# Scatters into expert bins: from pairs without a wait to one transfer at a time

## The chip, the cores and the metric

The kernel runs on one core of one Trainium2 chip. The metric is the device time in microseconds (us), taken as the median of several executions; the version before the change has 756.64 us, from three runs between 754.47 and 756.89.

## The reference

Two stages follow each other. The first filters each of 8 sequences of 2496 rows and 256 columns along its length in the frequency domain. The second sends each of the 19,968 filtered rows to one of eight experts.

```python
X = np.fft.rfft(x, axis=1)
y = np.fft.irfft(X * (filt_r + 1j * filt_i)[None], n=2496, axis=1)   # (8, 2496, 256)
x = y.reshape(19968, 256)
logits = x @ w_gate + modality_bias[modality_id]                     # 8 experts
e_idx = np.argmax(logits, axis=1)
gate_w = softmax(logits)[arange, e_idx]
for e in range(8):
    mask = e_idx == e
    h = np.maximum(x[mask] @ w1[e], 0.0)                             # 256 -> 1024
    out[mask] = gate_w[mask, None] * (h @ w2[e])                     # 1024 -> 256
```

## The kernel before

**The filter.** A sequence is a *group* `g`, 0 to 7. Its transform is cut into three stages of matrix products with data going through DRAM between them: `stage1` (input rows to `b1_d`), `stage2` (the other factor, the filter, and its inverse, to `b2_d`) and `stage3` (the last factor, into the tile `yw`). GpSimd loads the inputs (`load_x`, L125, four loads for a group), SyncE stores the results of the first two stages (L228, L454) and loads them again (L415, L422).

**The routing.** `stage3` leaves the rows of a group in `yw`, as 20 columns of 128 rows (the last two columns of 96), 520 bytes for a row: 256 values in 16 bits, the row's number and its gate. `count` and `place` compute the expert of each row and its place `pos` in that expert's bin. `yw` and `pos` have two buffers each. L463 writes the row numbers into a new `yw`.

**The bins.** `scatter(g, k)` writes two columns with two indirect transfers of GpSimd (L561), each taking the place of 128 rows from `pos`, into the DRAM tensor `bins_d`. Scatters are declared free of dependencies on each other and on loads written ahead of them. A load of the bins that is written after a scatter does wait for it.

**The experts.** The bins are read in 85 blocks of 256 rows of one expert. `load` brings a block in (`xs`, SyncE, L635), three blocks ahead; `turn` copies the expert's first weights (L651) and transposes the block (L661); `up` (L672, L676) and `down` (L684) compute it in four steps each, `down` of one block beside `up` of the next. After the last step of `down`, VectorE scales the result into `osb` (L691, three buffers), and GpSimd writes the rows to the output with two indirect transfers (L694). A call of `moe.step()` makes one step, so every fourth call issues an output pair.

**The order.** One loop over *slots* `n` writes the program. In each slot each stage of the groups that are under way advances by one piece; a group starts 14 slots after the one before it. Then one pair of scatters follows where a group is waiting for it in `to_bins`, and 2.25 expert steps on average. Twenty scatters thus take ten slots, and in the eleventh the group's blocks are opened for the experts. Groups have 1, 10, 10, 10, 9, 10, 10 and 25 blocks. The last group's blocks are opened after ends of bins have been padded (`pad_bins`, L709, SyncE). When the slots end, the rest of the blocks is computed without anything else beside it. The instructions of each engine are then ordered by when they are ready in the program's own planning, where a pin does not say otherwise: `behind("out", 1)` keeps a scatter behind the last output transfer written ahead of it. A pin is an order on the engine's queue and no wait.

```python
        if to_bins:
            g, k = to_bins[0]
            if k < NPY:
                scatter(g, k)
                to_bins[0][1] += 1
            else:
                if g == B - 1:
                    pad_bins()
                moe.open(tabs[g], KR[g], g == B - 1)
                to_bins.pop(0)
```

Of the kernel before, what the change touches and what calls it, by code (L numbers as in the profile page):

```python
# [17 lines left out]
IOA = bass.IndirectOffsetOnAxis  # L18
# [10 lines left out]
def kernel(  # L29
# [395 lines left out]
    def stage2(g, k):  # L425

        s = k * EV
        if s < NS:
            ps = pp.tile([P, EV, D], F32, tag="ps")
            for i in range(EV):  # L430
                nc.tensor.matmul(ps[:KB, i, :], lhsT=w2m[:, s + i, :], rhs=st[g]["t2", s // SCH][:, s % SCH + i, :],  # L431
                                 start=True, stop=True)
        if k > 0:
            s_ = s - EV
            p1, p2 = st[g]["p"]
            pz = pp.tile([P, EV, D], F32, tag="ps")
            for i in range(EV):
                nc.tensor.matmul(pz[:KB, i, :], lhsT=a1m[:, s_ + i, :], rhs=p1[:, i, :], start=True, stop=False)  # L438
                nc.tensor.matmul(pz[:KB, i, :], lhsT=a2m[:, s_ + i, :], rhs=p2[:, i, :], start=False, stop=True)  # L439
        if s < NS:  # L440
            sl = slice(s, s + EV)
            xf = rp.tile([KB, EV, D], BF16, tag="xf")
            nc.scalar.copy(xf, ps[:KB])  # L443
            p1 = rp.tile([KB, EV, D], BF16, tag="p1")
            nc.vector.tensor_mul(p1, xf, g1[:, sl, :])  # L445
            nc.vector.tensor_mul(xf, xf, g2[:, sl, :])  # L446
            st[g]["p"] = (p1, xf)
        if k > 0:
            kk = k - 1
            if kk % 2 == 0:  # L450
                st[g]["z"] = rp.tile([KB, 2, EV, D], BF16, tag="z", bufs=2, name="z")
            nc.scalar.copy(st[g]["z"][:, kk % 2], pz[:KB])  # L452
            if kk % 2 == 1:
                nc.sync.dma_start(b2_d[g, s - 2 * EV:s].rearrange("s p c -> p s c"),  # L454
                                  st[g]["z"].rearrange("p a b d -> p (a b) d"))

    def stage3(g, k):

        u0 = k * EV
        if k == 0:  # L460
            yw = yp.tile([P, NY, RW], I32, tag="yo", name="yo")
            st[g]["yw"] = yw
            nc.gpsimd.tensor_single_scalar(yw[:, :, DW:DW + 1], tok, g * S, op=ALU.add)  # L463
            lg = sp.tile([P, NY, E], F32, tag="lg", bufs=2)
            st[g]["lg"] = lg
            nc.vector.tensor_mul(lg, mids[:, g, :, None].to_broadcast([P, NY, E]),
                                 biasd[:, None, :].to_broadcast([P, NY, E]))
            nc.vector.tensor_add(lg, lg, bias0[:, None, :].to_broadcast([P, NY, E]))
        yo = st[g]["yw"].bitcast(BF16)
        if k < NPY:  # L470
            t0 = TCH[k // 3][0]
            t4 = st[g]["t4", k // 3]
            ps = pp.tile([P, EV, D], F32, tag="ps")
            for i in range(EV):
                a, b = divmod(u0 + i, 3)
                t, tc_, c0 = (4 * a + b, 4 * a + 3, b * KC) if u0 < NYF else (4 * NYG + i, 4 * NYG + 1, 0)
                nc.tensor.matmul(ps[:KA, i, :], lhsT=wbm, rhs=t4[:, t - t0, :], start=True, stop=True)  # L477
                nc.tensor.matmul(ps[KA:P, i, :], lhsT=wbm[:, c0:c0 + KC], rhs=t4[:, tc_ - t0, :],  # L478
                                 start=True, stop=True)

        ub, uc = u0 - EV, u0 - 2 * EV
        if k > 0:
            lt = pp.tile([P, 2 * D], F32, tag="ps")
            pT = lt[:, 0:D].bitcast(BF16).rearrange("p (i a q) -> p i a q", i=EV, a=DC)
            psL = lt[:, D:D + EV * E].rearrange("p (i e) -> p i e", e=E)
        if 0 < k <= NPY:
            for i in range(EV):
                for dc in range(DC):
                    nc.tensor.transpose(pT[:, i, dc, :], yo[:, ub + i, dc * P:(dc + 1) * P], ident)  # L489
        if k > 1:  # L490
            yT = st[g]["yT"]
            for i in range(EV):
                for dc in range(DC):
                    nc.tensor.matmul(psL[:, i, :], lhsT=yT[:, i, dc, :], rhs=wg[:, dc, :],
                                     start=(dc == 0), stop=(dc == DC - 1))
        if 0 < k <= NPY:
            st[g]["yT"] = sp.tile([P, EV, DC, P], BF16, tag="yT", bufs=2, name="yT")
            nc.vector.tensor_copy(st[g]["yT"], pT)  # L498
        if k < NPY:
            dst = yo[:, u0:u0 + EV, 0:D]  # L500
            if k % 2:
                nc.scalar.activation(dst, ps, AF.Copy, scale=1.0 / S)
            else:
                nc.vector.tensor_scalar_mul(dst, ps, 1.0 / S)
        if k > 1:
            lg = st[g]["lg"]
            nc.vector.tensor_add(lg[:, uc:uc + EV], lg[:, uc:uc + EV], psL)
# [46 lines left out]
        nc.vector.reduce_sum(ssum, lg, axis=AX.X)  # L554
        nc.vector.reciprocal(yw[:, :, DW + 1].bitcast(F32), ssum)

    def scatter(g, k):
        for t in range(k * EV, (k + 1) * EV):
            rows = P if t < NYF else KA
            with behind("out", 1):  # L560
                ins = nc.gpsimd.indirect_dma_start(  # L561
                    out=bins_d[:, :], out_offset=IOA(ap=st[g]["pos"][:rows, t:t + 1], axis=0),
                    in_=st[g]["yw"][:rows, t, :], in_offset=None)

            free_of(ins, "bins")
            free_of(ins, "bin_reads")
            tc.add_to_no_dep_group("bins", ins.ins)

    def free_of(ins, group):
        tc.declare_no_dep(ins.ins, group=group, reason="disjoint rows")  # L570
# [48 lines left out]

    binv = bins_d.rearrange("(n p i) d -> n p i d", p=P, i=NI)  # L620

    marks = {"ld": [], "up": [], "w1": [], "out": []}

    def behind(what, n):

        m = marks[what]
        return tc.issue_after(m[-n]) if len(m) >= n else nullcontext()
# [39 lines left out]
    def up(b, q):  # L667
        hps = hp.tile([P, FQ, NI * P], F32, tag="hps")
        for k in range(FQ):
            ft = q * FQ + k  # L670
            for dc in range(DC):
                mm = nc.tensor.matmul(hps[:, k, :], lhsT=b["w1"][:, dc, ft * P:(ft + 1) * P],  # L672
                                 rhs=b["xT"][:, dc].rearrange("p i t -> p (i t)"),
                                 start=(dc == 0), stop=(dc == DC - 1))
        marks["up"].append(mm.ins)
        nc.scalar.activation(b["hT"][:, q * FQ:(q + 1) * FQ, :], hps, AF.Relu)  # L676

    def down(b, q):
        if q == 0:
            b["ops"] = op.tile([P, NI, D], F32, tag="ops", bufs=2, name="ops")  # L680
        for k in range(FQ):
            ft = q * FQ + k
            for i in range(NI):
                nc.tensor.matmul(b["ops"][:, i, :], lhsT=b["hT"][:, ft, i * P:(i + 1) * P],  # L684
                                 rhs=w2sb[:, ds(b["ej"], 1), ft, :],
                                 start=(ft == 0 and i == 0), stop=(ft == FT - 1 and i == NI - 1))
        if (q + 1) * FQ == FT:
            osb = ep.tile([P, NI, D], F32, tag="osb", bufs=3)
            gate = b["meta"][:, :, 1:2].bitcast(F32)
            for i in range(NI):  # L690
                nc.vector.tensor_scalar_mul(osb[:, i, :], b["ops"][:, i, :], gate[:, i, :])  # L691
            for i in range(NI):
                kw = dict(bounds_check=N - 1, oob_is_err=False) if b["last"] else {}
                ins = nc.gpsimd.indirect_dma_start(  # L694
                    out=out[:, :], out_offset=IOA(ap=b["meta"][:, i, 0:1], axis=0),
                    in_=osb[:, i, :], in_offset=None, **kw)
                marks["out"].append(ins.ins)
                free_of(ins, "outs")
                tc.add_to_no_dep_group("outs", ins.ins)

# [69 lines left out]
    owed = 0.0  # L770


    GAP = NP + 1
    OFF2 = NP + 3
    OFF3 = OFF2 + NS // EV + 1 + 3
# [2 lines left out]
    while True:  # L778
# [9 lines left out]
        for g in range(B):  # L788
# [7 lines left out]
            if k == NPY + 3:  # L796
                place(g)
                tabs[g] = table(KR[g], g == B - 1)
                to_bins.append([g, 0])
        if to_bins:  # L800
            g, k = to_bins[0]
            if k < NPY:
                scatter(g, k)
                to_bins[0][1] += 1
            else:
                if g == B - 1:
                    pad_bins()
                moe.open(tabs[g], KR[g], g == B - 1)
                to_bins.pop(0)
        if (n - NP) % 4 == 0 and (n - NP) // 4 < E:  # L810
            load_w((n - NP) // 4)
        owed += STEPS
        while owed >= 1:
            owed -= 1
            moe.step()
        n += 1
        if not to_bins and n > (B - 1) * GAP + OFF3 + NPY + 4:
            break
# [32 lines left out]
```

## Time and profile before

| | |
|---|---|
| Median of the runs | 756.64 us |
| The profiled execution's own time | 879.74 us |
| Its span, first to last instruction | 878.0 us |
| Mean granted TensorE clock in it | 0.811 of full speed |
| Busy: TensorE, VectorE, ScalarE, GpSimd | 650.8, 385.7, 387.3, 367.7 us |
| Scatters (L561) | 160, 979 ns each on GpSimd |
| Output transfers (L694) | 170, 989 ns each on GpSimd |
| First scatter, last scatter issued | 151.3 us, 706.3 us |

The profile comes from one execution, which took 123 us longer than the median run. Durations are read from it and compared inside it; a time for the runs needs the step from one to the other. PE is TensorE's matrix products, PEld its weight loads, DVE VectorE, ACT ScalarE, POOL GpSimd and SP SyncE. A row of the groups gives line, engine, operation and tiles, the count, then busy time and mean duration in ns, then the idle time of the engine just ahead of such instructions and what ended most of it. SPq is SyncE's DMA queue, which does no arithmetic.

### The profile page before, as it was taken

To read this page: it belongs to the slowest core of one execution; us is meant where nothing else is said; L and a number is where in the kernel's file an instruction comes from. 1 tells how busy PE (TensorE), PEld (TensorE's weight loads), DVE (VectorE), ACT (ScalarE), POOL (GpSimd) and SP (SyncE) were. 2 spreads that over 40 slices of the span, in tenths; PEclk is the share of its full clock that TensorE was granted. 3 is DMA by queue.
4 is the path that set the end of the run, shared out by engine and by line. 5 is a ranking of instruction groups with operands and counts; after the bars stand their busy time and mean duration, and the time that the engine had idled before them with its cause. 6 is when DMAs were issued, how large, how long until landed. Compare 5 with 4: busy or idle time off the path is not lost.

```text
span 878.0 us, 15948 instructions
## 1 busy us (share of the span) xinstructions
PE 650.8 (74%) x4886; PEld 497.7 (57%) x4886; DVE 385.7 (44%) x1248; ACT 387.3 (44%) x695; POOL 367.7 (42%) x413
## 2 busy tenths in 40 slices
PE   1463678697596787787956886877694679999996
PEld 1352446465365556565744674665473457777775
DVE  5431235346255434553733464454253224444442
ACT  1553335345254444463724543452242235555553
POOL 5131201625505433544345345435546544444444
PEclk9985555557579878897969899897897769999998
DMA  8799986566465446454533343342222223222320
GB/s 154 162 223 211 225 176 159 130 139 173 105 149 149 121 100 160 119 149 100 168 110 112 100 115 117 88 127 71 70 73 95 95 79 101 94 92 92 96 64 1
DMA packets 92696, 106.80 MB, mean 122 GB/s; under 512 B 12708, under 2 KB 75754, under 8 KB 92460
## 3 DMA queue, kind: packets, MB, share of 16 engines
q0 software_dynamic: 29120, 50.75, 24.8%
q1 hardware_dynamic: 63496, 55.03, 23.9%
q8 instruction: 44, 0.72, 0.4%
q14 instruction: 36, 0.29, 0.1%
HBM read 71.87 MB, written 54.31 MB: 144 GB/s over the span
## 4 chain that ended last, share of the span: by engine, by line
PE 23%; issue 17%; POOL 8%; another core or an unknown queue 4%; DMA 4%; DVE 3%; ACT 2%; POOLq 0%; SPq 0%; DVEq 0%; ACTq 0%
PE hps L672 7%; PE ops L684 6%; POOL out_dram L694 6%; DMA out_dram<-osb,meta 2%; PE ps L478 2%; POOL bins_d L561 2%; PE ps L477 2%; PE lt L489 1%; DMA bins_d<-yo,pos_i 1%; ACT hT L676 1%; PE ps L431 1%; PE pT L661 1%; PE pz L439 1%; PE pz L438 1%
## 5 line engine op out<-in xcount | busy, mean ns | idle before, releaser
L676 ACT ACTIVATE hT<-hps 128x512 f16<-128x512 f32 x340 | 197.4, 597 | 282.1 <-PE hps L672 131.6
L694 POOL DMA_INDIRECT out_dram<-osb,meta x170 | 168.1, 989 | 269.0 <-DVE osb L691 220.3
L672 PE MATMUL hps<-xT,w 128*128 128x256 f16 x1360 | 231.4, 293 | 32.8 <-ACT hT L676 16.5
L684 PE MATMUL ops<-w2sb,hT 128*128 x1360 | 226.6, 289 | 9.8 <-issue 9.3
L561 POOL DMA_INDIRECT bins_d<-yo,pos_i x160 | 156.7, 979 | 58.3 <-issue 47.3
L684 PEld LDWEIGHTS <-hT 128*128 128x128 f16 x1360 | 141.2, 104 | 45.2 <-issue 18.4
L672 PEld LDWEIGHTS <-w 128*128 128x128 f16 x1360 | 131.9, 104 | 61.2 <-issue 24.8
L225 ACT CAST t<-ps 96x512 f16<-96x512 f32 x104 | 59.7, 583 | 92.5 <-PE ps L222 31.6
L651 DVE COPY w<-w1sb 128x2048 f16 x85 | 59.2, 697 | 63.4 <-PE ops L684 46.7
L477 PE MATMUL ps<-t,wbm 96*96 96x256 f16 x160 | 56.8, 355 | 40.4 <-ACT t L225 18.8
L662 DVE COPY xT<-pT 128x512 f16<-128x512 f16 x85 | 35.9, 423 | 112.2 <-remote 39.9
L445 DVE TENSOR_TENSOR p<-xf,g 104x512 f16<-104x512 f16 x96 | 40.6, 423 | 96.4 <-ACT xf L443 80.3
L691 DVE TENSOR_SCALAR osb<-ops,meta 128x256 f32<-128x256 f32 x170 | 74.9, 477 | 15.6 <-PE ops L684 9.4
L222 PE MATMUL ps<-xt,w1m 96*96 96x256 f16 x208 | 53.3, 358 | 36.0 <-DVE w1m L205 16.7
L125 POOL DMA_DIRECT2D xt<-in_x_dram x32 | 18.9, 590 | 143.4 <-PE ps L222 117.4
L431 PE MATMUL ps<-t,w2m 104*104 104x256 f16 x192 | 48.4, 344 | 40.4 <-issue 12.0
L498 DVE COPY yT<-lt 128x512 f16<-128x512 f16 x80 | 33.8, 422 | 94.2 <-remote 43.5
L438 PE MATMUL pz<-p,a1m 104*104 104x256 f16 x192 | 62.4, 338 | 16.1 <-ACT t L225 5.9
L452 ACT CAST z<-pz 104x512 f16<-104x512 f32 x96 | 56.7, 590 | 34.5 <-PE pz L439 9.5
L443 ACT CAST xf<-ps 104x512 f16<-104x512 f32 x96 | 56.4, 587 | 23.2 <-PE ps L431 15.5
L439 PE MATMUL pz<-xf,a2m 104*104 104x256 f16 x192 | 62.9, 341 | 1.3 <-DVE xf L446 1.1
L489 PE MATMUL lt<-ident,yo 128*128 128x128 f16 x320 | 40.2, 264 | 24.4 <-ACT xf L443 16.6
(185 smaller groups left out, 632.1 us busy)
## 6 DMA issues: line engine op xcount, KB each, us to landing
xs<-bins_d SPq DMA_DIRECT2D x85, 130.0 KB
t<-b_d SPq DMA_DIRECT2D x24, 416.0 KB
b_d<-z SPq DMA_DIRECT2D x48, 208.0 KB
xt<-in_x_dram POOLq DMA_DIRECT2D x24, 384.0 KB
b_d<-t SPq DMA_DIRECT2D x48, 192.0 KB
t<-b_d SPq DMA_DIRECT2D x24, 384.0 KB
w1sb<-in_moe_w_dram POOLq DMA_DIRECT2D x8, 512.0 KB
w2sb<-in_moe_w_dram POOLq DMA_DIRECT2D x8, 512.0 KB
```

The source lines that it names most:

```text
L225: nc.scalar.copy(st[g]["t1"][:, k % 2], ps[:KA])
L431: nc.tensor.matmul(ps[:KB, i, :], lhsT=w2m[:, s + i, :], rhs=st[g]["t2", s // SCH][:, s % SCH + i, :], start=True, stop=True)
L438: nc.tensor.matmul(pz[:KB, i, :], lhsT=a1m[:, s_ + i, :], rhs=p1[:, i, :], start=True, stop=False)
L439: nc.tensor.matmul(pz[:KB, i, :], lhsT=a2m[:, s_ + i, :], rhs=p2[:, i, :], start=False, stop=True)
L477: nc.tensor.matmul(ps[:KA, i, :], lhsT=wbm, rhs=t4[:, t - t0, :], start=True, stop=True)
L561: ins = nc.gpsimd.indirect_dma_start(out=bins_d[:, :], out_offset=IOA(ap=st[g]["pos"][:rows, t:t + 1], axis=0), in_=st[g]["yw"][:rows, t, ...
L651: cp = nc.vector.tensor_copy(b["w1"].rearrange("p a f -> p (a f)"), w1sb[:, ds(ej, 1)].rearrange("p o a f -> p (o a f)"))
L672: mm = nc.tensor.matmul(hps[:, k, :], lhsT=b["w1"][:, dc, ft * P:(ft + 1) * P], rhs=b["xT"][:, dc].rearrange("p i t -> p (i t)"), start=(d ...
L676: nc.scalar.activation(b["hT"][:, q * FQ:(q + 1) * FQ, :], hps, AF.Relu)
L684: nc.tensor.matmul(b["ops"][:, i, :], lhsT=b["hT"][:, ft, i * P:(i + 1) * P], rhs=w2sb[:, ds(b["ej"], 1), ft, :], start=(ft == 0 and i == ...
L691: nc.vector.tensor_scalar_mul(osb[:, i, :], b["ops"][:, i, :], gate[:, i, :])
L694: ins = nc.gpsimd.indirect_dma_start(out=out[:, :], out_offset=IOA(ap=b["meta"][:, i, 0:1], axis=0), in_=osb[:, i, :], in_offset=None, **kw)
```

## The change

Each scatter call now issues one column, and each scatter gets a dependency on the indirect transfer written just ahead of it, a scatter or an output transfer (`follow`, over the list `marks["sc"]`): it is issued only when that transfer has landed. Outputs enter the list but get no such dependency themselves. The scatters of a slot are spread: one at its head and one after each expert step that issued no output, at most two in a slot. From the slot on in which the last group is placed, the limit is 20. The list `marks["pe"]` is filled by three places and read by none.

```diff
-    def scatter(g, k):
-        for t in range(k * EV, (k + 1) * EV):
-            rows = P if t < NYF else KA
-            with behind("out", 1):
-                ins = nc.gpsimd.indirect_dma_start(
-                    out=bins_d[:, :], out_offset=IOA(ap=st[g]["pos"][:rows, t:t + 1], axis=0),
-                    in_=st[g]["yw"][:rows, t, :], in_offset=None)
...
+    def scatter(g, t):
+
+        rows = P if t < NYF else KA
+        with behind("out", 1):
+            ins = nc.gpsimd.indirect_dma_start(
+                out=bins_d[:, :], out_offset=IOA(ap=st[g]["pos"][:rows, t:t + 1], axis=0),
+                in_=st[g]["yw"][:rows, t, :], in_offset=None)
+
+        free_of(ins, "bins")
+        free_of(ins, "bin_reads")
+        tc.add_to_no_dep_group("bins", ins.ins)
+        follow(ins)
+
+    def follow(ins):
+
+        if marks["sc"]:
+            tc.add_manual_dep(ins.ins, marks["sc"][-1].name,
+                              mybir.DependencyInfo(mybir.DependencyClass.Sync, mybir.DependencyReason.DATA),
+                              reason="one in flight")
+        marks["sc"].append(ins.ins)
...
-    marks = {"ld": [], "up": [], "w1": [], "out": []}
+    marks = {"ld": [], "up": [], "w1": [], "out": [], "pe": [], "sc": []}
...
                 marks["out"].append(ins.ins)
+                marks["sc"].append(ins.ins)
...
+    def pace(left):
+
+        if to_bins and left:
+            g, t = to_bins[0]
+            if t < NY:
+                scatter(g, t)
+                to_bins[0][1] += 1
+                left -= 1
+            else:
+                if g == B - 1:
+                    pad_bins()
+                moe.open(tabs[g], KR[g], g == B - 1)
+                to_bins.pop(0)
+        return left
...
+        left = 2 if n < (B - 1) * GAP + OFF3 + NPY + 3 else NY
+        left = pace(left)
         if (n - NP) % 4 == 0 and (n - NP) // 4 < E:
             load_w((n - NP) // 4)
         owed += STEPS
         while owed >= 1:
             owed -= 1
+            outs = len(marks["out"])
             moe.step()
+            if len(marks["out"]) == outs:
+                left = pace(left)
```

More of the change, by code (lines that the diff above doesn't have):

```diff
@@ L430, in stage2 @@
             for i in range(EV):
-                nc.tensor.matmul(ps[:KB, i, :], lhsT=w2m[:, s + i, :], rhs=st[g]["t2", s // SCH][:, s % SCH + i, :],
-                                 start=True, stop=True)
+                mm = nc.tensor.matmul(ps[:KB, i, :], lhsT=w2m[:, s + i, :],
+                                      rhs=st[g]["t2", s // SCH][:, s % SCH + i, :], start=True, stop=True)
+            marks["pe"].append(mm.ins)
         if k > 0:
@@ L477, in stage3 @@
                 nc.tensor.matmul(ps[:KA, i, :], lhsT=wbm, rhs=t4[:, t - t0, :], start=True, stop=True)
-                nc.tensor.matmul(ps[KA:P, i, :], lhsT=wbm[:, c0:c0 + KC], rhs=t4[:, tc_ - t0, :],
-                                 start=True, stop=True)
+                mm = nc.tensor.matmul(ps[KA:P, i, :], lhsT=wbm[:, c0:c0 + KC], rhs=t4[:, tc_ - t0, :],
+                                      start=True, stop=True)
+            marks["pe"].append(mm.ins)
         ub, uc = u0 - EV, u0 - 2 * EV
@@ L555, in place @@
         nc.vector.reciprocal(yw[:, :, DW + 1].bitcast(F32), ssum)
-    def scatter(g, k):
-        for t in range(k * EV, (k + 1) * EV):
-            rows = P if t < NYF else KA
-            with behind("out", 1):
-                ins = nc.gpsimd.indirect_dma_start(
-                    out=bins_d[:, :], out_offset=IOA(ap=st[g]["pos"][:rows, t:t + 1], axis=0),
-                    in_=st[g]["yw"][:rows, t, :], in_offset=None)
-            free_of(ins, "bins")
-            free_of(ins, "bin_reads")
-            tc.add_to_no_dep_group("bins", ins.ins)
+    def scatter(g, t):
[14 more added lines that the diff above has]
+        marks["sc"].append(ins.ins)
     def free_of(ins, group):
@@ L675, in up @@
         marks["up"].append(mm.ins)
+        marks["pe"].append(mm.ins)
         nc.scalar.activation(b["hT"][:, q * FQ:(q + 1) * FQ, :], hps, AF.Relu)
@@ L799 @@
                 to_bins.append([g, 0])
[L800 to L809, printed above, removed]
+        left = 2 if n < (B - 1) * GAP + OFF3 + NPY + 3 else NY
+        left = pace(left)
         if (n - NP) % 4 == 0 and (n - NP) // 4 < E:
```

## The prediction

> **What bounds the kernel now.** I read the busy line of the page first, then the windows by stage, then the rows of the two indirect transfers, then GpSimd's and SyncE's waits.
>
> ```profile
> PE 650.8 (74%) x4886; PEld 497.7 (57%) x4886; DVE 385.7 (44%) x1248; ACT 387.3 (44%) x695; POOL 367.7 (42%) x413
> ...
> L694 POOL DMA_INDIRECT out_dram<-osb,meta x170 | 168.1, 989 | 269.0 <-DVE osb L691 220.3
> ...
> L561 POOL DMA_INDIRECT bins_d<-yo,pos_i x160 | 156.7, 979 | 58.3 <-issue 47.3
> ```
>
> No engine is full: TensorE leads with 74%, GpSimd (POOL) is at 42%. A scatter into the bins (L561) holds POOL 0.98 us and is preceded by nothing but "issue" (0.30 us each): today it waits for no transfer. The windows (busy us of PE, PEld, DVE, ACT, POOL, each with a count; then clock, DMA share, GB/s) show where PE is not fed:
>
> ```profile
> 500.00:600.00 100.00, 77.41 (x659) 61.61 (x658) 54.71 (x189) 45.27 (x81) 44.72 (x47) 0.91 0.38 112
> 600.00:660.00 60.00, 45.12 (x360) 32.43 (x358) 24.54 (x77) 19.17 (x34) 31.48 (x33) 0.83 0.22 69
> 660.00:712.00 52.00, 27.84 (x194) 20.45 (x193) 15.75 (x55) 12.74 (x22) 30.22 (x31) 0.71 0.29 92
> 712.00:800.00 88.00, 84.09 (x742) 69.47 (x740) 40.91 (x103) 46.71 (x82) 39.48 (x42) 0.98 0.29 92
> ```
>
> While the last group is scattered (660 to 712) PE is busy 27.8 of 52 us; after the last scatter, 84 of 88. So scatters already set PE's pace there. The link is SyncE's (SPq) wait: a block's load reads the bins and waits until every scatter written ahead of it in the program has landed. The waits of SPq, then the chain in order of time (start, us, what), first around the third group's end, then in the last group:
>
> ```profile
> SPq L635 <- DMA bins_d<-yo,pos_i: 71.9, 20, 8.0
> ```
>
> ```profile
> 331.67 6.99 DMA bins_d<-yo,pos_i
> ...
> 342.40 2.33 DMA xs<-bins_d
> ...
> 345.40 1.04 PE hps L672 x4
> ```
>
> ```profile
> 670.95 2.28 DMA bins_d<-yo,pos_i
> ...
> 673.50 0.97 POOL out_dram L694
> ```
>
> Twenty loads waited 71.9 us for scatters; in the middle piece the load, and then PE, wait for one. The last piece gives the price: 2.28 us from issue to landing, and POOL goes on 0.27 us later (673.23 to 673.50). POOL's timeline shows today's spacing:
>
> ```profile
> 357.44 1.21 POOL L561 DMA_INDIRECT bins_d<-yo,pos_i  x1 [1.20 <-DVE m L594]
> 358.95 0.97 POOL L561 DMA_INDIRECT bins_d<-yo,pos_i  x1 [0.30 <-issue]
> 360.22 0.97 POOL L561 DMA_INDIRECT bins_d<-yo,pos_i  x1 [0.30 <-issue]
> 361.50 0.97 POOL L561 DMA_INDIRECT bins_d<-yo,pos_i  x1 [0.30 <-issue]
> 362.77 1.02 POOL L694 DMA_INDIRECT out_dram<-osb,meta  x1 [0.30 <-issue]
> 364.10 0.97 POOL L694 DMA_INDIRECT out_dram<-osb,meta  x1 [0.31 <-issue]
> 365.38 0.97 POOL L561 DMA_INDIRECT bins_d<-yo,pos_i  x1 [0.30 <-issue]
> ```
>
> Issue to issue is 1.27 us, so about two are in flight. In the trace's packets, a scatter's last data packet ends 1.88 us after issue in the quicker quarter, 2.30 us on the mean of 160.
>
> **What the Trainium skill says.** "DMA: Bandwidth & Descriptors", section "Anatomy of one DMA — SWDGE (gpsimd) path", gives about 2.0 us fixed plus bytes/436e3 for a GpSimd DMA, most of it the write receipt. For a scatter (128 rows of 520 bytes, 66,560) that is 2.15 us; the trace has 2.28, and agrees. For an output transfer (131,072 bytes) it is 2.30; the chain has 3.58 us (from 719.07), and the measurement is used. The same page, "Rules for kernel authors", says to issue early and wait on the semaphore late, so that the fixed cost overlaps. The change does the reverse for these transfers.
>
> **The change part by part.**
>
> 1. *The wait.* Nothing is added in instructions or bytes; 160 scatters get a wait on POOL. Behind another scatter, the distance grows from 1.27 to 2.28 + 0.27 = 2.55 us at best; with the mean packet end (2.30 + 0.40 + 0.27) 2.97. I take 2.8. Behind an output, 3.58 + 0.27 = 3.85 us from that output's issue, unless other POOL work fills it.
> 2. *POOL in one steady group.* A group is 14 slots; from the first scatter of the third group (270.3) to that of the eighth (664.4) it takes 78.8 us in the profiled execution. The median run is 756.64/879.74 = 0.860 of that execution, so 67.8 us at its pace. Today POOL needs 20 × 1.27 + 16 outputs × 1.27 + 4 input loads × 0.87 = 49 us. After: ten slots hold 22.5 steps, so 5.6 output pairs, and 14.4 scatters follow a scatter. 14.4 × 2.8 = 40.3; the 5.6 scatter-pair-scatter stretches take 3 × 1.27 = 3.8 us each where the pair goes into a wait that exists anyway (21.3); the remaining 2.3 pairs and the input loads 9.3. Sum **71 us**. It fits into 78.8 and exceeds 67.8 by 3. If each wait behind an output is met in full, 5.6 × (2 × 1.27 + 3.85) = 35.8 replaces 21.3: **85 us**.
> 3. *What queues behind.* Behind a waiting scatter on POOL stand the outputs (three osb buffers let PE run about three blocks ahead) and the input loads at L125. On the other side, SPq's block loads wait for the scatters, and behind them on SPq stand the FFT's stores (L228, L454) and loads (L415, L422). Scatters take 61.6 of a group's 71 us where they had ten slots, 48 us at the median's pace: 13 us late, under three blocks' 26 us, but the 20 waits of 71.9 us lengthen. I price a steady group at 5 us (3 of POOL, 2 of SPq) in a range of 0 to 17; five groups: **+25**.
> 4. *The first two groups.* No outputs are mixed in: today 27.4 and 25.5 us of scatters, after 20 × 2.8 = 56. The first block and the next ten come some 29 us later each. Cover: the FFT work, which can run ahead. From 0 to 29 each; I take 10: **+20**.
> 5. *The last group.* No cover: PE has 27.8 us of work in 52. Today its scatters run from 664.4 to 707.2. After, about 15.5 × 2.8 + 4 × 3.8 = 59 us, 16 more, with one block less passed meanwhile (+4): **+20**, between 0 and 30.
> 6. *The placing.* One per step instead of a pair per slot, none after a step that issues outputs; in the last group up to three per slot. No instruction is added; the rate stays two per slot elsewhere, so nothing by itself. The matmul marks are read by nothing: zero.
>
> Sum: +65 us. Against the profiled execution (879.74) items 4 and 5 stay and item 3 shrinks to 2 per group, some +50, near 930. Against the median of the runs: 756.6 + 65 = **822 us**. Own range 785 to 860.
>
> **The rivals.**
>
> *Full waits.* Every scatter behind an output holds POOL idle until that output has landed. Groups need 85 us against 67.8: +17 × 5, with 29 × 2 at the start less some cover (30) and 30 at the end: +145, **900 us**. For: the diff puts outputs into the chain. Against: outputs are free to be ordered ahead of a waiting scatter; the trace shows POOL work moved to where it is ready (L463 stands right behind a group's last scatter).
>
> *Hidden.* The order of the queues already spaces the scatters out, and blocks are in stock: **757 us**. For: POOL is idle 58% of the span. Against: SPq's 71.9 us of waits, and the bursts at 1.27 us.
>
> *Faster.* Bursts of four scatters hold back an output pair by 4 × 1.27 = 5.1 us, which in 660 to 712 leaves PE 24 us idle. If spread scatters let outputs pass, and the last group's blocks open three slots earlier, up to those 24 us come back: **733 us**. It decides if the scatters of the last group end no later than today, so at under 43/20 = 2.1 us each; the cheapest wait measured is 2.55.
>
> *The wait isn't there.* If a landed transfer is never ahead, distances stay 1.27 and the time 757. The explicit dependency speaks against.
>
> **How the numbers follow.** Slow-down of item sums 0.60; full waits 0.22; hidden or no wait 0.06; faster 0.12. A measurement of this kernel tells about 0.3% (2.3 us) from no change; so faster 0.12, same 0.05, slower 0.83. The range takes in the likeliest case, hidden at its lower edge and full waits at its upper: 755 to 905.
>
> **What would show it.** Right: in POOL's timeline scatters 2.5 to 3 us apart, idle before them ended by the transfer ahead; L561's idle time up from 58 to some 250 us; SPq L635 waiting well over 72 us for bins; the last group's scatters over 55 us. Wrong: scatters still 1.27 us apart, or spaced with SPq's wait for bins unchanged and the 660 to 712 stretch no longer. Full waits would show as output-landing waits ahead of scatters summing to over 100 us.

## The result, and the profile after

The changed kernel takes 765.01 us (762.88 to 767.98, four runs) against 756.76 us (754.47 to 757.99, four runs): a ratio of 1.0115, 95% interval 1.0073 to 1.0157. A second comparison on another occasion gave 1.0162 (1.0107 to 1.0217), so the change costs 1 to 2%, some 8 to 13 us. That is slower, as forecast, but by only an eighth to a fifth of the 65 us in the sum.

The profiled execution that the prediction reads (879.74 us) ran at another pace than the timed runs of the same kernel. A second profile of that kernel took 748.95 us with a span of 747.2 us. All comparisons of profiles below are with the second one, which is called "before, second profile". What slowed the first is not known; its effect on the forecast is told further down.

The busy line and the rows of the two indirect transfers, changed kernel:

```profile
PE 617.4 (81%) x4886; PEld 485.3 (63%) x4886; DVE 381.2 (50%) x1248; ACT 394.8 (52%) x695; POOL 372.8 (49%) x413
...
L706 POOL DMA_INDIRECT out_dram<-osb,meta x170 | 167.2, 984 | 162.2 <-DVE osb L703 113.4
...
L563 POOL DMA_INDIRECT bins_d<-yo,pos_i x160 | 161.6, 1010 | 78.0 <-issue 38.2
```

The counts are those of before, and the busy times are close to those of the second profile (TensorE 605.0 us, GpSimd 372.5). POOL idles 78.0 us ahead of scatters (L563), where the prediction expected some 250 with 160 real waits. The view of the tile `bins_d` says what ended that idle time (us, times), and how long a scatter takes to land:

```profile
  issue: 38.2, 123
  DMA out_dram<-osb,meta: 17.6, 14
...
  DMA bins_d<-yo,pos_i: 1.2, 4
...
DMA to landing us min/median/max: 2.2/2.6/5.6
```

Before 123 of the 160 scatters POOL waited for nothing but its own issue. An output's landing ended the idle time 14 times, a scatter's landing 4 times, for 1.2 us in all. The same view of the kernel before (second profile) shows which of the two is new:

```profile
  DMA bins_d<-yo,pos_i: 1.2, 4
...
  DMA out_dram<-osb,meta: 0.3, 1
```

The 1.2 us behind scatters stand there too, without any dependency; the waits behind outputs are new. POOL's timeline of the changed kernel agrees:

```profile
461.03 0.96 POOL L563 DMA_INDIRECT bins_d<-yo,pos_i  x1 [0.30 <-issue]
462.30 0.96 POOL L563 DMA_INDIRECT bins_d<-yo,pos_i  x1 [0.31 <-ACT hT L688]
463.56 0.96 POOL L563 DMA_INDIRECT bins_d<-yo,pos_i  x1 [0.30 <-issue]
464.82 0.96 POOL L563 DMA_INDIRECT bins_d<-yo,pos_i  x1 [0.30 <-issue]
466.09 1.02 POOL L706 DMA_INDIRECT out_dram<-osb,meta  x1 [0.30 <-issue]
467.41 0.96 POOL L706 DMA_INDIRECT out_dram<-osb,meta  x1 [0.31 <-issue]
468.68 0.95 POOL L563 DMA_INDIRECT bins_d<-yo,pos_i  x1 [0.30 <-issue]
...
502.03 0.96 POOL L706 DMA_INDIRECT out_dram<-osb,meta  x1 [0.30 <-issue]
504.84 0.91 POOL L563 DMA_INDIRECT bins_d<-yo,pos_i  x1 [1.85 <-DMA out_dram<-osb,meta]
```

Four scatters in a row are still 1.27 us apart, with a landing time of 2.2 us at the least: two are in flight, and "one in flight" does not happen. Even the scatter at 468.68 follows its output pair without a wait; only the last line shows one that had to wait. The built program lists the semaphores that each instruction waits for, and agrees: 38 scatters carry a wait for an output transfer, none has one for the scatter ahead of it. In a scatter's definition stands, three lines above `follow`, the declaration that scatters are free of each other. So the change as described above is what the code asks for with `follow`, and not what is built: of the dependencies of 160 scatters only 38 became waits, all of them on outputs.

Before, second profile: SyncE's and DVE's waits.

```profile
SPq L635 <- DMA bins_d<-yo,pos_i: 168.4, 47, 13.3
```

```profile
DVE meta L657 <- DMA xs<-bins_d: 104.5, 42, 8.0
```

Changed kernel:

```profile
SPq L646 <- DMA bins_d<-yo,pos_i: 177.2, 39, 7.9
```

```profile
DVE meta L668 <- DMA xs<-bins_d: 133.2, 43, 7.6
```

SyncE waits about as long for scatters as before. Beside the 71.9 us of the first profile, the 177.2 us would have looked like the prediction's sign "well over 72"; at the usual pace the kernel before already has 168.4. VectorE waits 29 us longer for blocks. The windows of the last group and around it, before (second profile) and changed kernel:

```profile
562.00:598.00 36.00, 22.32 (x186) 17.89 (x184) 11.99 (x36) 12.33 (x21) 27.77 (x28) 0.86 0.36 115
598.00:747.00 149.00, 136.85 (x1309) 121.69 (x1308) 74.69 (x181) 86.18 (x145) 77.68 (x80) 0.99 0.29 89
```

```profile
577.00:611.00 34.00, 22.13 (x179) 17.85 (x178) 10.59 (x34) 11.57 (x20) 26.19 (x26) 0.90 0.34 110
611.00:766.00 155.00, 143.45 (x1337) 126.61 (x1335) 76.48 (x185) 88.12 (x148) 78.95 (x81) 0.95 0.29 89
```

The last group is scattered in 34 us instead of 36, with about as much PE work, and leaves a little more for the stretch behind it. Its scatters, which the prediction had made 16 us longer, are not. Most of the lateness arises in the groups before: the table gives the issue of each group's first scatter and of the very last one, in us from the start, and the span. It is read from POOL's timelines. The two spans of before and changed kernel are 19 us apart, where the medians of the runs are 8 to 13 apart: the second profile of before caught one of its quicker executions (748.95 us), and that of the changed kernel the slowest of its four (767.98 us). Single differences of a few us in this table are no more than rough.

| | g0 | g1 | g2 | g3 | g4 | g5 | g6 | g7 | last scatter | span |
|---|---|---|---|---|---|---|---|---|---|---|
| before, second profile | 149.9 | 201.0 | 252.8 | 323.1 | 390.5 | 450.4 | 507.6 | 561.9 | 598.4 | 747.2 |
| placing alone | 150.6 | 202.1 | 255.4 | 324.4 | 388.8 | 447.7 | 504.9 | 558.7 | 592.2 | 748.5 |
| changed kernel | 150.4 | 205.0 | 259.4 | 326.4 | 395.4 | 461.0 | 520.9 | 577.1 | 611.2 | 766.2 |
| all behind outputs | 150.4 | 205.4 | 259.5 | 333.4 | 408.2 | 482.4 | 550.1 | 610.9 | 649.0 | 801.8 |
| two in flight | 149.2 | 205.7 | 267.1 | 339.1 | 409.2 | 472.3 | 535.5 | 594.1 | 635.9 | 787.3 |
| real chain | 149.9 | 240.6 | 324.0 | 401.4 | 483.0 | 560.1 | 634.5 | 701.9 | 761.5 | 911.3 |
| chain from the third group, second time | 150.6 | 202.2 | 256.4 | 338.3 | 419.5 | 497.3 | 570.2 | 639.4 | 699.4 | 840.7 |

### The profile page after: what moved, and what is told of

It is laid out like the page before. It is cut to its first block, busy times and chain, and to the rows that moved or that the text cites. A ratio compares the mean times of both kernels' runs of the same rounds, so it can differ in the third digit from the quotient of the medians.

```text
span 766.2 us, 15941 instructions
## 1 busy us (share of the span) xinstructions
PE 617.4 (81%) x4886; PEld 485.3 (63%) x4886; DVE 381.2 (50%) x1248; ACT 394.8 (52%) x695; POOL 372.8 (49%) x413
## 5 line engine op out<-in xcount | busy, mean ns | idle before, releaser
L688 ACT ACTIVATE hT<-hps 128x512 f16<-128x512 f32 x340 | 202.7, 597 | 193.2 <-PE hps L683 191.2
L683 PE MATMUL hps<-xT,w 128*128 128x256 f16 x1360 | 221.7, 284 | 32.1 <-DVE xT L673 31.0
L696 PE MATMUL ops<-w2sb,hT 128*128 x1360 | 215.0, 282 | 0.3 <-issue 0.3
L563 POOL DMA_INDIRECT bins_d<-yo,pos_i x160 | 161.6, 1010 | 78.0 <-issue 38.2
L683 PEld LDWEIGHTS <-w 128*128 128x128 f16 x1360 | 127.6, 101 | 54.6 <-DVE xT L673 32.4
L696 PEld LDWEIGHTS <-hT 128*128 128x128 f16 x1360 | 137.8, 101 | 22.4 <-issue 0.6
L668 DVE COPY meta<-xs 128x4 int32<-128x4 int32 x85 | 15.6, 183 | 150.0 <-DMA xs<-bins_d 133.2
L222 PEld LDWEIGHTS <-w1m 96*96 96x96 f16 x208 | 28.5, 159 | 38.8 <-issue 20.3
L479 PE MATMUL ps<-t,wbm 96*32 96x256 f16 x160 | 52.9, 330 | 0.0
```

The lines of the kernel that those rows point to most:

```text
L222: nc.tensor.matmul(ps[:KA, i, :], lhsT=w1m, rhs=xt[:, t - t0 + i, :], start=True, stop=True)
L563: ins = nc.gpsimd.indirect_dma_start(out=bins_d[:, :], out_offset=IOA(ap=st[g]["pos"][:rows, t:t + 1], axis=0), in_=st[g]["yw"][:rows, t, ...
```

## The experiments

My theory after the result: the dependency of a scatter on a scatter never became a wait; the 38 waits behind outputs make the 1.2%, and the new placing nothing. The rivals: the placing makes it, or real waits are simply cheap.

**The kernel before again** (`before_again`, no edit).

> The kernel before, unchanged, for a second profile: the first profiled execution took 879.74 us where the runs have 757. If that execution was an exception, the span here is 755 to 760 us, groups start some 60 us apart (78.8 in the first), and SyncE's waits for the bins can be compared with the changed kernel's 177.2 us. If profiling slows this kernel as such, the span is near 880 again. Ratio 1.000 within 0.004 on either.

Measured: span 747.2 us, ratio 0.998 (0.994 to 1.002). From g2 to g7 a group takes (561.9 - 252.8) / 5 = 61.8 us, where the first profile had 78.8. So a profile of this kernel need not be slow. The first profile was at another pace.

**The placing alone** (`placing_only`).

```diff
         tc.add_to_no_dep_group("bins", ins.ins)
-        follow(ins)
```

> The changed kernel with the call of follow left out: the new placing of the scatters, no dependency. If the waits behind output transfers make the changed kernel's 1.2%, this is at 1.000 (0.997 to 1.004), some 757 us. If the placing makes it (the order written, the last group's limit of 20), it is at 1.010 to 1.014, some 765 us, and the waits cost nothing.

Measured: ratio 0.999 (0.996 to 1.002). The placing alone costs and gives nothing; the call of `follow`, of which only the waits behind outputs are built, makes the slow-down. A dependency also enters the planning that orders the queues, so the runs show the cost of both together and not of the waits apart from the order.

**The dependency alone** (`wait_only`): `follow` stays, the pairs of before come back.

```diff
+                left = 0
         return left
...
-        left = 2 if n < (B - 1) * GAP + OFF3 + NPY + 3 else NY
-        left = pace(left)
+        left = 2
+        left = pace(left)
+        left = pace(left)
...
-            outs = len(marks["out"])
             moe.step()
-            if len(marks["out"]) == outs:
-                left = pace(left)
```

> The dependency of the changed kernel with the placing of before: pairs of scatters at the head of a slot, none after steps, ten slots for the last group too. If the waits make the 1.2%: 1.008 to 1.014, some 764 us. If the placing makes it: 0.998 to 1.003, some 757 us. Either way scatters stay 1.27 us apart, since a scatter's dependency on a scatter does not become a wait as long as scatters are declared free of each other.

Measured: 775.57 us, ratio 1.026 (1.020 to 1.031). Confirmed in kind: the dependency slows the kernel without the new placing, and scatters that follow each other directly keep a median distance of 1.28 us. The size was not expected: 2.6%, where the changed kernel has 1.2% and, the second time, 1.6%, with 37 waits instead of 38 and 18.9 us of POOL's idle time behind outputs instead of 17.6. The interval touches that of the changed kernel's second comparison (1.0107 to 1.0217), so that the spread placing softens the waits is suggested and not sure, and how it would do so stays open.

**A real chain** (`real_chain`): the declaration goes, and each scatter waits for the one ahead.

```diff
-        free_of(ins, "bins")
         free_of(ins, "bin_reads")
-        tc.add_to_no_dep_group("bins", ins.ins)
         follow(ins)
```

> The changed kernel without the declaration that scatters are free of each other, so that each scatter does wait until the scatter ahead of it has landed. The prediction's price of a real wait: scatters 2.5 to 3 us apart, SyncE's waits for the bins well above 177 us, and +65 us, so 822 us or a ratio of 1.087 (1.04 to 1.14). If the wait is hidden where scatters have room in their slots: at most 1.02, below 772 us, with the distances grown all the same.

Measured: 913.8 us, ratio 1.214 (1.206 to 1.222). The program now lists 154 waits for scatters. Its `bins_d` view and its timeline:

```profile
  DMA bins_d<-yo,pos_i: 186.1, 93
```

```profile
568.85 1.22 POOL L563 DMA_INDIRECT bins_d<-yo,pos_i  x1 [0.30 <-issue]
571.67 0.97 POOL L563 DMA_INDIRECT bins_d<-yo,pos_i  x1 [1.60 <-DMA bins_d<-yo,pos_i]
...
589.88 0.97 POOL L563 DMA_INDIRECT bins_d<-yo,pos_i  x1 [0.30 <-issue]
593.25 0.97 POOL L563 DMA_INDIRECT bins_d<-yo,pos_i  x1 [2.39 <-DMA bins_d<-yo,pos_i]
```

```profile
SPq L644 <- DMA bins_d<-yo,pos_i: 331.5, 57, 19.9
```

Scatters that follow each other directly stand 3.49 us apart on the mean of 88 (median 3.06), and SyncE waits twice as long for them. This is the mechanism that the prediction had costed, and it costs 157 us, not 65.

**The chain without the outputs** (`chain_no_out`): `real_chain` without its line `follow(ins)`.

> Each scatter waits for the scatter ahead of it; output transfers are not in the chain (real_chain, 1.214, without its outputs). If the latency of one scatter after the other sets the time, little changes: 1.18 to 1.22, 890 to 920 us, scatters still over 2.5 us apart. If the waits behind outputs carry a large part of the 157 us: 1.08 to 1.15.

Measured: 907.27 us, ratio 1.203 (1.195 to 1.210). The latency of one scatter after the other carries nearly all of it. The outputs in the chain add about a hundredth at most; the two intervals overlap.

**Two in flight** (`chain_two`): two lists of scatters, each free of the other.

```diff
-        free_of(ins, "bins")
+        free_of(ins, "bins%d" % ((t + 1) % 2))
         free_of(ins, "bin_reads")
-        tc.add_to_no_dep_group("bins", ins.ins)
-        follow(ins)
+        tc.add_to_no_dep_group("bins%d" % (t % 2), ins.ins)
```

> As chain_no_out, but each scatter waits for the scatter two ahead, so two are in flight. By the latency theory the cheapest distance is half of 2.55 us, so about the 1.27 us that POOL takes anyway: most of the cost goes, 1.01 to 1.05, 765 to 795 us. If the cost is in the waits as such (the queue standing still, the order that is planned around them), it keeps over half of the slow-down: 1.10 or more.

Measured: 789.97 us, ratio 1.048 (1.041 to 1.054); direct distances 1.75 us on the mean. Three quarters of the cost of the chain go with the second transfer in flight, as the latency reading had it. The value is at the upper edge of the expected: the direct distances did not come down to 1.27 us, and POOL still waited for scatters 35 times, 42.6 us in all.

**Every scatter behind the last output** (`all_behind_out`).

```diff
-        follow(ins)
+        if marks["out"]:
+            tc.add_manual_dep(ins.ins, marks["out"][-1].name,
+                              mybir.DependencyInfo(mybir.DependencyClass.Sync, mybir.DependencyReason.DATA),
+                              reason="behind the last output")
```

> The placing of the changed kernel; every scatter, not the first alone, depends on the last output transfer ahead of it, and none on a scatter. In the changed kernel the one waiting scatter of a burst mostly stands fourth, when the output has landed. Here none can go first, so each burst waits some 2.4 us: if moving the wait to the end of the burst is what made the change cheap, this is at 1.03 to 1.08, 780 to 817 us, with over 60 us of POOL waiting for outputs. If not, it is near the changed kernel's 1.012.

Measured: 802.56 us, ratio 1.062 (1.055 to 1.069), and POOL's timeline:

```profile
490.18 0.96 POOL L709 DMA_INDIRECT out_dram<-osb,meta  x1 [0.30 <-issue]
495.82 1.16 POOL L563 DMA_INDIRECT bins_d<-yo,pos_i  x1 [4.68 <-DMA out_dram<-osb,meta]
497.29 0.96 POOL L563 DMA_INDIRECT bins_d<-yo,pos_i  x1 [0.30 <-issue]
```

This lies in the range of the first reading; POOL's idle time behind outputs is 57.4 us, a little under the 60 expected. The burst starts with the wait, and 27 of 31 direct steps from an output to a scatter exceed 2 us (mean 3.69). In the changed kernel it is 5 of 33, mean 1.63. There one scatter of a burst has the dependency and the others are free to go ahead of it on the queue. By the built programs, both kernels have 38 scatters with a wait for an output. Here 35 of them stand first behind the outputs; in the changed kernel 9 stand first, 4 second, 9 third, 13 fourth and 3 fifth, when the outputs have mostly landed. This is why the change costs 1 to 2% and not 6%. It is not all: in `wait_only` 21 of the 37 stand fourth or fifth, more than the changed kernel's 16, and it still costs more.

**Blocks brought in five ahead** (`before_ahead5`), on the kernel before.

```diff
-        xs = ep.tile([P, NI, RW], I32, tag="xs", bufs=5)
+        xs = ep.tile([P, NI, RW], I32, tag="xs", bufs=7)
...
-            while self.todo and len(self.ready) < 3:
+            while self.todo and len(self.ready) < 5:
```

> The kernel before with the blocks brought in five ahead instead of three (xs has seven buffers instead of five): a load then stands behind fewer scatters. SyncE's waits of 168 us for the bins and DVE's 105 us for blocks should fall by a third or more. If late blocks cost PE time in the kernel before, 0.975 to 0.995, 738 to 753 us; if they are covered, 0.997 to 1.003.

Measured: 825.14 us, ratio 1.093 (1.087 to 1.098). Neither reading held. SyncE's waits for bins fell to 160.3 us only, and the stretch behind the last scatter took 203 us instead of 149, where VectorE waited for outputs to land (111.7 us, 31 times in that stretch, against 12.5 us, 12 times, in the kernel before; 146.4 us in the whole run). Those waits are for a free buffer of `meta`, which the output transfers read and of which the edit left eight. A new wait covers what was to be measured, so this run says nothing on late blocks.

**The first two groups without the chain** (`chain_from_third`).

```diff
+        if g < 2:
+            free_of(ins, "bins")
         free_of(ins, "bin_reads")
+        tc.add_to_no_dep_group("bins", ins.ins)
-        follow(ins)
+        if g >= 2:
+            follow(ins)
+        else:
+            marks["sc"].append(ins.ins)
```

> real_chain with the first two groups' scatters free of each other again. In real_chain the starts of the second and third group come 40 and 31 us later than in the kernel before, and the profile shows two waits of some 30 us of stage3's results for a free yw tile. If those are the cost of the first two groups, some 71 us of the 157 go: 835 to 855 us, 1.10 to 1.13. If the later groups only take over the lateness (they are bound by the chain of scatters anyway), under 30 us go and it stays above 880 us, 1.17.

Measured: 875.79 us, beside 876.95 us for the kernel before in 15 runs at the pace of its first profile; ratio 0.999 (0.994 to 1.003). At that pace a group of the kernel before took 78.8 us in the first profile, and the chain costs nothing. This pair answers nothing about the usual pace, so it was taken again.

> The same kernel as chain_from_third, taken again because the kernel before ran at another pace beside it (877 us, as in its first profiled execution, instead of 757). At the usual pace of 757: 835 to 855 us, 1.10 to 1.13, if the first two groups carry 71 of real_chain's 157 us; above 880 us, 1.17, if the later groups take over the lateness. At the pace of 877 again: a ratio of 1.00, since a chain of scatters at 3 us then fits into the longer slots.

Measured: 842.33 us beside 753.23, ratio 1.118 (1.112 to 1.123): 71 us less than `real_chain`, or 68 when each is set against the kernel before beside it, as the first reading said. The waits of `real_chain` name what held the first two groups (`yo` is the profile's name for `yw`):

```profile
PE lt L491 <- DVE yo L506: 65.9, 3, 32.5
...
ACT yo L504 <- DMA bins_d<-yo,pos_i: 65.6, 4, 32.3
DVE yo L506 <- DMA bins_d<-yo,pos_i: 56.3, 3, 31.8
```

VectorE and ScalarE cannot write `stage3`'s results for group g + 2 until group g's scatters have left their `yw`; PE stands behind them for up to 32.5 us at a time. Without the chain in the first two groups, one such wait for scatters is left, of 3.8 us. A third `yw` buffer would try this directly; it was not tried.

**The changed kernel again** (`after_again`).

> The changed kernel once more beside the kernel before: 1.008 to 1.016 if its 1.2% come from the 38 waits behind outputs at the usual pace of 757 us; 0.995 to 1.005 if this pair runs at the pace of 877 us, where the slots are longer and such waits are covered.

Measured: 766.2 us beside 753.23, ratio 1.016 (1.011 to 1.022), at the upper edge of the expected for the usual pace. In its profile stand again 39 of SyncE's waits for bins with 183.7 us, and 10 waits of scatters for outputs with 15.1 us.

## Why the prediction was right and wrong

*Item 1, the wait: wrong, and this is the step that failed.* "160 scatters get a wait on POOL" should have been 38, those behind outputs; scatters stayed 1.27 us apart, where the text took 2.8. The diff itself shows why: `free_of(ins, "bins")` stays ahead of `follow`. `real_chain` shows it by taking the declaration away. The rival "the wait isn't there" was half the truth, and the sentence against it ("the explicit dependency speaks against") was where the argument stopped reading. Where the wait is real, its price was near the median and a fifth below the mean: 2.8 us taken, 3.06 and 3.49 measured. The landing after an output was taken too long: 3.58 us from one piece of the chain, where the second profile has a median of 2.6. The estimate of 2.30 from the Trainium skill ("DMA: Bandwidth & Descriptors", "Anatomy of one DMA — SWDGE (gpsimd) path") was nearer.

*Item 2, POOL in one group: right for a real chain, irrelevant for the change.* `real_chain` takes (701.9 - 324.0) / 5 = 75.6 us for a group, between the 71 and the 85 of the text. What it is compared with was wrong: 0.860 was applied to a whole execution, but the extra time of that execution lay mostly in the groups: of 131 us between the two spans, 5 × (78.8 - 61.8) = 85 are in these five. A group of the kernel before takes 61.8 us, not 67.8.

*Item 3, the five groups: 25 us predicted.* For the real chain the table gives 7 + 14 + 17 + 17 + 13 = 69 us, or 75.6 - 61.8 = 14 for a group, where the text has 71 - 67.8 = 3 and 2 more for SyncE's loads; the wrong pace is the larger part of the difference. For the change it gives -3 + 2 + 6 + 3 + 2 = 9 us, from its few waits. The path named does occur: at this place the critical chain of the changed kernel runs from a scatter's landing to the block's load and VectorE (start, us, what).

```profile
498.99 2.78 DMA bins_d<-yo,pos_i
501.88 2.08 DMA xs<-bins_d
504.16 0.33 DVE xT L673
```

*Item 4, the first two groups: 20 us predicted.* The real chain pays 40 + 32 = 71 us, more than the 29 each that the text allowed at most. "The FFT work, which can run ahead" was the mistake: by the waits of `real_chain` it can until `stage3` needs a `yw`, of which there are two. The prediction had the two buffers in the description of the kernel and not in the sum. For the change these groups cost 3.5 + 2.6 us.

*Item 5, the last group: 20 us predicted.* The real chain pays 23 + 1 = 24. The change pays nothing in the group (-2.4) and 6 us behind it, which the placing alone has too (8 us, given back earlier).

*Item 6, the placing: right*, 0.999. Together with the dependency it may do more than was said, as `wait_only` costs 2.6% without it; what that is stays open.

The sum of 65 us was thus too small for the mechanism that it described, by a factor of 2.4, and far too large for the change, because that mechanism is built for a quarter of the scatters, and for most of these behind others that cover it. "Full waits" (900 us) is near the 913.8 of `real_chain`, but by luck: it charged waits behind outputs, which end only 5.7 us of POOL's idle time ahead of scatters there, and `chain_no_out`, which has none, still takes 907.27. "Faster" failed as argued; the last group gained 2 us.

## What to carry to other kernels

Before a dependency is costed, check that it becomes a wait: here a declaration of independence on the same instruction took it away, and the distances of issues in the timeline tell it at a glance. Where a wait stands on a queue can matter more than how many there are: with 35 of 38 waits at the head of their bursts the cost was 6%, with 9 of 38 there 1 to 2%, though `wait_only` shows that this is not all. When transfers are made to follow each other, list every buffer that they hold, with the number of its copies; here the waits name the two copies of `yw` for the first two groups, which carried some 70 of 157 us. And take the pace of a stage from that stage: a factor over the whole execution put the slack of a group at 6 us too much.

## What the runs showed that was not expected

One transfer more in flight took the chain from a ratio of 1.203 to 1.048. The same kernel, without any edit, ran at 757 us in most comparisons and at 877 us in one, in all 15 runs there, as in its first profile; in that profile the groups took longer and the stretch behind them was 172 instead of 149 us. In that condition a chain of scatters from the third group on cost nothing (0.999), where it costs 1.118 otherwise. The two profiles at the slower pace, the first of before and the first of `chain_from_third`, have rows that none of the other profiles has: waits whose end the profile puts down to nothing that it recorded ("remote"):

```profile
ACT hT L676 <- remote: 60.2, 14, 8.1
```

```profile
ACT t L225 <- remote: 25.7, 8, 4.5
```

The DMA packets themselves are not slower: by the busy shares of the two DMA queues, 24.8 and 23.9% of 878.0 us in the first profile and 28.8 and 28.6% of 747.2 us in the second, they took the same time, 428 and 429 us. What sets the two paces is not settled by these runs.
